# A hand-written planner for VectorE: exponential passes admitted by the next step's work, and side work held until the evacuation in front of it is due to end

## The chip, the core and the metric

The kernel runs on one core of a Trainium2 chip, as one launch. Its time is the device time of that launch in microseconds (us); for a kernel the median over its runs is given. The core's engines are TensorE (PE in the profile, its weight loads PEld), VectorE (DVE), ScalarE (ACT), GpSimd (POOL) and SyncE (SP); SP and POOL issue the DMAs.

## What is computed

Two rounds of an attention block and a token-mixing MLP, with residuals, on x of 2048 tokens by 640 features in bf16:

```python
def _A_ref(x, wqkv, wo):                 # H = 32 heads of 20
    qkv = transpose(reshape(x @ wqkv, (B, S, 3, H, Dh)), (2, 0, 3, 1, 4))
    q, k, v = qkv[0], qkv[1], qkv[2]
    scores = einsum("bhqd,bhkd->bhqk", q, k) * (Dh ** -0.5)
    o = einsum("bhqk,bhkd->bhqd", softmax(scores), v)
    return reshape(transpose(o, (0, 2, 1, 3)), (B, S, D)) @ wo

def _B_ref(x, w1, b1, w2, b2):           # mixes tokens: S = 2048, F = 1536
    u = gelu(einsum("bsd,sf->bdf", layernorm(x), w1) + b1)
    return transpose(einsum("bdf,fs->bds", u, w2) + b2, (0, 2, 1))

x = x + _A_ref(layernorm(x), wqkv, wo)
x = x + _B_ref(layernorm(x), w1, b1, w2, b2)
...                                      # both once more, same weights
```

The exponentials of the softmax are the bulk: 32 heads x 2048 x 2048 of them in each of the two attention blocks.

## The kernel before

**Score blocks and steps.** In `attention` (L257) a unit is a query block of 512 (qb, four of them), a group of four heads (g, eight) and a key block of 128 (kt, sixteen). A unit has four score blocks of 128 x 512, one for each head. Most of them get their exponential on ScalarE. Some get it on VectorE (`on_ve`, L290): all four of each group's last key block, and in some groups two of the one before, 166 blocks in each layer. A step is one tile of three score blocks in PSUM, in a pool with two buffers. It is either three blocks for ScalarE (a full step) or two for ScalarE and one for VectorE in the third place (a short step). There are 683 steps in each layer.

**The loop** (L751) is written out by hand and runs over the steps. In step t it emits the score matmuls of step t + 1 (`emit_S`, L441) and, if that step is short, VectorE's first read of the third block (`ve_first`, L351, tile ew). It then emits ScalarE's exponential of step t (`emit_exp`, L474, tile P), the multiplications with V of the units that are ready (`emit_PV`, L683, accumulator acc), the side work, and VectorE's passes. The order of TensorE's instructions is fixed to the order of emission. That of the other engines is not: the framework's scheduler puts together each engine's queue from what it reckons to be ready, with the emission order as priority.

**VectorE's exponential.** Two ew reads make a pair of 128 x 1024. `ve_enqueue` (L358) adds four passes for it to the list `ve_chain`: ey (L368, planned at 0.69 us), et (L374), Pd in its cubic form (L381) and Pd with the exponent added (L386), the last three planned at 1.22 us each. `ve_step` (L398), at the end of each step, advances a planned clock by the step's length (0.92 us for a short one, 1.344 for a full one) and emits passes from the list. The planner keeps `free`, the time until which VectorE is planned to be busy; every VectorE piece that the loop emits adds its cost to it (`dve_cost`, L345). A unit with blocks of VectorE has its multiplication with V deferred until its passes are planned to be done or nothing else is left; `ve_flush` (L411) then emits any pass still missing.

**Normalisation.** After the last unit of a group, `normalize` (L481) emits four VectorE instructions: a transpose out of the accumulator (T, L486), a reciprocal (rden), a product (T again) and a transpose into attnT (L493); it is planned at 2.4 us. The accumulator has one buffer, so the next group's first multiplication with V waits for the first transpose.

**Side work** is a queue of groups of matmuls that use one PSUM bank (tile misc, one buffer), each ended by a VectorE evacuation planned at 0.28 to 0.7 us: projections of keys and queries for later groups (L240, evacuated at L642 into KT and QTq), the output projection (L579, L614; evacuated at L589, L622 and L627 with the residual, into xin, x1s or x1last), and the part of the MLP's first product that belongs to the rows already finished (key "M", L551; evacuated at L557 into ustg and added to uacc in DRAM by a DMA that POOL issues, L560 and L562; its weights w1st are loaded by SP). `emit_fills` (L700) emits matmuls of it up to a budget a step; after each group it pauses for one step (`cooldown`). `planned_fill` (L730) tells at the start of a step whether there will be side work; if not, `keep_busy` (L460) emits matmuls with zero weights into the accumulator (L464). Side work that a group of heads needs at once is forced by `ensure_ready` (L663).

**After the loop** what is left of the side work is emitted with the score tile's pool as its bank (`tail_alloc`, L773). Then comes the layer norm of the last four row blocks (`emit_ln2_staged`, L520: statistics and nmr on VectorE, rstd on POOL at L182, hh on ScalarE and VectorE). `mixer_mm1` (L785) multiplies these rows (L826, tile big), adds uacc, which SP loads into ua (L809, four buffers), and `mixer_mm2` (L851) makes the second product from weights w2s (SP, L848), with x1in (SP, L886) as the residual.

Of the kernel before, what the change touches and what calls it, by code (L numbers as in the profile page):

```python
# [29 lines left out]
CFG = dict(  # L30
    SLOTS=4,
    FILL_NOPV=3.0,
    FILL_PV=1.5,
    PV_LAGT=1,
    PT_BUFS=4,
    FILL_GAP=1,
    KQ_AHEAD=1,
    A0_LAG=2,
    VE_SPACING=(2, 3),
    VE_LEAD=8,  # L40
    VE_SLACK=0.3,
)

LOG2E = 1.4426950408889634
# [8 lines left out]
def kernel(  # L53
# [203 lines left out]
    def attention(st, x_in_ap, x_mid, uacc_l):  # L257
        layer = st.layer
        KT, hT = st.KT, st.hT
        with ExitStack() as p1:  # L260
# [22 lines left out]
            fill_state = dict(cur=None, idx=0, tile=None, cooldown=0, unit=0)  # L283
# [11 lines left out]
            tiles, loc, last_tile = [], {}, {}  # L295
# [8 lines left out]
            while act_chunks or ve_left:  # L304
                t = len(tiles)
# [26 lines left out]
            NTILES = len(tiles)  # L332
            tile_left = {t: len(acts) for t, (acts, _) in enumerate(tiles)}
            pv_count = {}
            pv_plain = [deque() for _ in range(NU // NKT)]
            pv_mixed = [deque() for _ in range(NU // NKT)]
# [5 lines left out]
            ve_chain = deque()  # L342
            ve_clock = dict(now=0.0, free=0.0)

            def dve_cost(us):  # L345
                ve_clock["free"] = max(ve_clock["free"], ve_clock["now"]) + us
# [45 lines left out]
            def ve_next():  # L392
                p, cost, fn = ve_chain.popleft()
                fn()
                dve_cost(cost)
                ve_ready[p] = ve_clock["free"]

            def ve_step(us):  # L398
                ve_clock["now"] += us
                while ve_chain and ve_clock["free"] <= ve_clock["now"] + CFG["VE_SLACK"]:  # L400
                    ve_next()

            def ve_need(n):
# [41 lines left out]
            def emit_S(t):  # L445
                acts, ve = tiles[t]
                for (n, j) in acts:
                    if j == HORDER[0]:
                        on_unit_start(n)
                St = sps.tile([128, 3, 512], F32, name="S")  # L450
                S_tiles[t] = St
                for i, (n, j) in enumerate(acts):
                    s_matmul(St, i, n, j)
                if ve is not None:
                    if units[ve[0]][0:2] != units[acts[0][0] if acts else ve[0]][0:2]:
                        ensure_ready(*units[ve[0]][0:2])
                    s_matmul(St, 2, ve[0], ve[1])
                    ve_first(*loc[ve], St)

            def keep_busy(count):  # L460
                for acc in acc_tiles.values():
                    for _ in range(count):
                        for j in range(4):
                            pe(nc.tensor.matmul(acc[32 * j:32 * j + 32, :], lhsT=zw[:], rhs=zr[:].to_broadcast([128, 4, 128]), start=False,  # L464
                                                stop=False, skip_group_check=True, tile_position=(0, 32 * j)))

            def emit_exp(t):
                St = S_tiles.pop(t)
                ncs = len(tiles[t][0])
                if ncs == 0:  # L470
                    return
                P = ptp.tile([128, 3, 512], BF16, name="P")
                P_tiles[t] = P
                ex = nc.scalar.activation(out=P[:, 0:ncs, :].rearrange("p a b -> p (a b)"),  # L474
                                     in_=St[:, 0:ncs, :].rearrange("p a b -> p (a b)"),
                                     func=ACT.Exp, scale=SCALE)
                other = ve_reader.pop(id(St), None)
                if other is not None:
                    tc.declare_no_dep(ex.ins, other.ins, reason="both only read the score tile, in different banks")
# [191 lines left out]
            def emit_PV(n):  # L671
                qb, g, kt = units[n]
                done = pv_count.get((qb, g), 0)
                pv_count[(qb, g)] = done + 1
                if done == 0:
                    acc_tiles[(qb, g)] = accp.tile([128, 512], F32, name="acc")
                acc = acc_tiles[(qb, g)]
                ve_flush(n)
                for j in range(4):
                    ti, slot = loc[(n, j)]  # L680
                    P = ve_P[ti] if on_ve(n, j) else P_tiles[ti]
                    hh = 4 * g + j
                    pe(nc.tensor.matmul(acc[32 * j:32 * j + 32, :],  # L683
                                        lhsT=Vaug[:, (kt * H + hh) * VW:(kt * H + hh) * VW + 32],
                                        rhs=P[:, slot, :], start=(done == 0), stop=(done == NKT - 1),
                                        tile_position=(0, 32 * j)))
                    if not on_ve(n, j):
                        tile_left[ti] -= 1
                        if tile_left[ti] == 0:
                            del P_tiles[ti]  # L690
                if done == NKT - 1:
                    normalize(qb, g, acc_tiles.pop((qb, g)))
                    dve_cost(2.4)
                    if qb == LASTQB and PARTIAL_LAST:
                        if g % 2 == 1:
                            enqueue_outproj_partial(qb, g)
                    elif g == NG - 1:
                        enqueue_outproj(qb)

            def emit_fills(budget, pool_alloc):  # L700
                fs = fill_state
                if fs["cooldown"] > 0:
                    fs["cooldown"] -= 1
                    return 0.0
                spent = 0.0
                while spent < budget:
                    if fs["cur"] is None:
                        if not fill_queue:
                            break
                        if fill_queue[0].get("not_before", 0) > fs["unit"] and budget < 100:  # L710
                            break
                        fs["cur"] = fill_queue.popleft()
                        fs["idx"] = 0
                        fs["tile"] = pool_alloc()
                    grp = fs["cur"]
                    grp["mms"][fs["idx"]](fs["tile"])
                    spent += grp["cost"][fs["idx"]]
                    fs["idx"] += 1
                    if fs["idx"] == len(grp["mms"]):
                        grp["evac"](fs["tile"])  # L720
                        dve_cost(grp.get("dve", 0.69))
                        fs["cur"] = None
                        fs["cooldown"] = CFG["FILL_GAP"]
                        break
                return spent
# [2 lines left out]
                return miscp.tile([128, 512], F32, name="misc")  # L728

            def planned_fill():  # L730
                if fill_state["cooldown"] != 0:
                    return False
                if fill_state["cur"] is not None:
                    return True
                return len(fill_queue) > 0 and fill_queue[0].get("not_before", 0) <= fill_state["unit"]

            LAGT = CFG["PV_LAGT"]
            pv_group = 0

            def pv_next(t, n_pv):  # L740
                if pv_group >= len(pv_plain):
                    return None
                plain, mixed = pv_plain[pv_group], pv_mixed[pv_group]
                if plain and last_tile[plain[0]] <= t - LAGT:
                    return plain.popleft()
                if mixed and last_tile[mixed[0]] <= t - LAGT and len(plain) < NKT - 3:
                    if not plain or (n_pv == 0 and ve_done(mixed[0])):
                        return mixed.popleft()
                return None
            emit_S(0)  # L750
            for t in range(NTILES):  # L751
                has_fill = planned_fill()
                if t + 1 < NTILES:
                    emit_S(t + 1)
                emit_exp(t)
                n_pv = 0
                while (n := pv_next(t, n_pv)) is not None:
                    emit_PV(n)
                    n_pv += 1
                    if not pv_plain[pv_group] and not pv_mixed[pv_group]:  # L760
                        pv_group += 1
                short = len(tiles[t][0]) < 3
                if not has_fill:
                    keep_busy(CFG["SLOTS"] - 1 - n_pv - short)
                emit_fills(CFG["FILL_PV"] if n_pv or short else CFG["FILL_NOPV"], misc_alloc)
                ve_step(0.92 if short else 1.344)
            in_attention[0] = False
            while (n := pv_next(NTILES + LAGT, 0)) is not None:
                emit_PV(n)
# [245 lines left out]
```

## Time and profile before

| what | value |
|---|---|
| median of 3 runs | 2021.24 us (2020.55 to 2022.6) |
| the profiled execution | 2025.45 us, span 2023.7 us |
| mean granted TensorE clock | 0.975 |
| first attention loop, first start to last end of L474 | 49.6 to 931.5 us |
| second attention loop | 1052.6 to 1937.3 us |
| VectorE's passes L368, L374, L381, L386 | 166 of each; 0.69, 1.22, 1.21 and 1.21 us mean |
| ew, L351 | 332, 0.68 us mean |
| T out of the accumulator, L486 | 64, 0.71 us mean |
| zero matmuls, L464 | 5232 |

In the profile a group reads "line engine operation out<-in", count, busy time and mean duration of one in ns, and behind a second bar the idle time of its engine just before it, with what ended most of that. A wait reads "who <- for whom: total us, times, longest". A row of a timeline has its start and its duration in us; what stands in square brackets is the engine's idle time before it and what ended it. Durations come from one execution; matmul durations overlap, as one starts before the last has ended.

### The profile page before, as it was taken

The page shows a single profiled execution, that of the slowest core. Times are in us where ns is not written, and L with a number is a line of the kernel's source. Part 1 is how long each engine was busy: PE and PEld are TensorE (multiplying, and loading weights), DVE is VectorE, ACT ScalarE, POOL GpSimd, SP SyncE. Part 2 cuts the span into 40 slices and gives each one's busy share as a digit, 9 for nine tenths or more (in the row PEclk, how much of TensorE's full clock was granted, in tenths as well). Part 3 has the DMA queues.
Part 4 walks back from the last instruction along what each step waited for, and adds up shares of the span by engine and source line. Part 5 has one row for each costly group of instructions (what it writes and reads, how often), then busy time and mean ns, then how long its engine had stood idle before and what let it go on. Part 6 is the DMA issues. An engine that isn't in the chain of part 4 may idle for free.

```text
span 2023.7 us, 39147 instructions
## 1 busy us (share of the span) xinstructions
PE 1723.9 (85%) x16395; PEld 615.5 (30%) x16592; DVE 1388.9 (69%) x2091; ACT 1801.0 (89%) x1504; POOL 155.1 (8%) x220
## 2 busy tenths in 40 slices
PE   7888888888888887887998888888888888878879
PEld 4222222232222222223542222222222222222235
DVE  6777787666766577773557787777657765767742
ACT  5999999999999999996349999999999999999952
POOL 2000000110012001110000000001000220011000
PEclk9999999999999999998999999999999999999989
DMA  6000000110134012214620000112101430233145
GB/s 135 1 1 1 1 19 26 67 49 8 34 67 68 1 40 45 42 21 136 207 83 1 1 1 1 34 33 69 38 14 40 79 56 2 59 51 43 15 149 185
DMA packets 90768, 97.34 MB, mean 48 GB/s; under 512 B 9696, under 2 KB 68192, under 8 KB 90592
## 3 DMA queue, kind: packets, MB, share of 16 engines
q1 hardware_dynamic: 70464, 71.22, 11.3%
q0 software_dynamic: 20128, 23.62, 7.8%
q8 instruction: 129, 2.11, 0.4%
q14 instruction: 47, 0.39, 0.1%
HBM read 55.48 MB, written 39.32 MB: 47 GB/s over the span
## 4 chain that ended last, share of the span: by engine, by line
ACT 34%; PE 23%; DVE 22%; issue 19%; DMA 1%; POOL 0%; SPq 0%; another core or an unknown queue 0%; ACTq 0%; DVEq 0%; POOLq 0%
ACT P L474 34%; PE S L441 6%; PE y L897 5%; DVE ew L351 4%; PE acc L683 3%; DVE et L374 3%; DVE Pd L381 3%; PE acc L464 2%; DVE ey L368 2%; DVE Pd L386 2%; PE pp L231 2%; DVE T L486 1%; PE misc L551 1%; PE misc L240 1%; DVE T L491 1%
## 5 line engine op out<-in xcount | busy, mean ns | idle before, releaser
L474 ACT ACTIVATE P<-S 128x1536 bf16<-128x1536 f32 (+1 forms) x1366 | 1709.1, 1447 | 58.5 <-PE S L441 43.9
L441 PE MATMUL S<-QTq,KT 32*128 32x512 bf16 x4096 | 574.6, 388 | 198.9 <-ACT P L474 137.9
L683 PE MATMUL acc<-P,Vaug 128*32 128x512 bf16 x3764 | 388.9, 396 | 27.3 <-DVE T L486 26.6
L351 DVE TENSOR_SCALAR ew<-S 128x512 int32<-128x512 f32 x332 | 226.1, 681 | 262.6 <-PE S L441 262.3
L441 PEld LDWEIGHTS <-KT 32*128 32x128 bf16 x4096 | 195.9, 91 | 689.0 <-issue 539.0
L464 PE MATMUL acc<-zr,zw 128*32 128x512 bf16 x5232 | 404.4, 388 | 0.0
L374 DVE SCALAR_TENSOR_TENSOR et<-ey 128x1024 f32<-128x1024 f32 x166 | 202.5, 1220 | 4.4
L386 DVE SCALAR_TENSOR_TENSOR Pd<-ew,Pd 128x1024 int16<-128x1024 int16 x166 | 201.3, 1213 | 2.4
L381 DVE SCALAR_TENSOR_TENSOR Pd<-et,ey 128x1024 bf16<-128x1024 f32 x166 | 200.6, 1208 | 1.6
L683 PEld LDWEIGHTS <-Vaug 128*32 128x32 bf16 x4096 | 108.1, 93 | 278.3 <-issue 278.1
L464 PEld LDWEIGHTS <-zw 128*32 128x32 bf16 x5232 | 128.8, 97 | 97.2 <-issue 41.0
L557 DVE COPY ustg<-misc 128x512 f32<-128x512 f32 (+1 forms) x144 | 69.4, 482 | 109.1 <-PE misc L551 89.6
L182 POOL TENSOR_TENSOR rstd<-veps,mhalf 128x1 f32<-128x1 f32 x64 | 38.9, 608 | 1168.9 <-DVE veps L177 1049.7
L562 POOL DMA_DIRECT2D uacc<-ustg x96 | 86.2, 899 | 435.0 <-DVE ustg L557 421.6
L368 DVE TENSOR_SCALAR ey<-ew 128x1024 f32<-128x1024 uint16 x166 | 114.8, 692 | 2.9
L551 PE MATMUL misc<-h2st,w1st 128*128 128x128 bf16 (+1 forms) x512 | 104.7, 300 | 6.6 <-DVE ustg L557 5.3
L897 PE MATMUL y<-uT,w2s 128*128 128x128 bf16 (+1 forms) x754 | 106.8, 298 | 3.8 <-ACT uT L840 3.1
L240 PE MATMUL misc<-hh,wq_pad 128*128 128x512 bf16 x268 | 84.9, 384 | 6.2 <-DVE KT L642 2.5
L240 PE MATMUL misc<-hh,wk_pad 128*128 128x512 bf16 x250 | 78.6, 388 | 6.9 <-DVE KT L642 5.0
L486 DVE STREAM_TRANSPOSE T<-acc 128x512 f32<-128x512 f32 x64 | 45.5, 711 | 55.5 <-PE acc L683 55.5
L579 PE MATMUL misc<-wo_pad,attnT 128*128 128x128 bf16 (+1 forms) x362 | 73.6, 303 | 2.0 <-issue 1.0
L897 PEld LDWEIGHTS <-w2s 128*128 128x128 bf16 x768 | 59.7, 98 | 49.4 <-issue 4.6
(86 smaller groups left out, 898.8 us busy)
## 6 DMA issues: line engine op xcount, KB each, us to landing
uacc<-ustg POOLq DMA_DIRECT2D x72, 256.0 KB, 4.0
w2s<-in_B_w_dram SPq DMA_DIRECT2D x16, 768.0 KB
w1st<-in_B_w_dram SPq DMA_DIRECT2D x36, 256.0 KB
x1in<-xd SPq DMA_DIRECT2D x24, 320.0 KB
ua<-uacc SPq DMA_DIRECT2D x24, 320.0 KB
xd<-x2s SPq DMA_DIRECT2D x16, 320.0 KB
xin<-xd SPq DMA_DIRECT2D x16, 320.0 KB
uacc<-ustg POOLq DMA_DIRECT2D x72, 64.0 KB, 2.8
```

The lines of the kernel that those rows point to most:

```text
L240: pe(nc.tensor.matmul(t[:, :], lhsT=wpad[:, dt_, g, :], rhs=st.hT[:, dt_, tb * 512:(tb + 1) * 512], start=(dt_ == 0), stop=(dt_ == NDT - 1)))
L351: first = nc.vector.tensor_scalar(out=ve_w[p][:, slot, :], in0=St[:, 2, :], scalar1=ve_scale * 65536.0, scalar2=-127.0 * 65536.0, op0=ALU. ...
L368: nc.vector.tensor_scalar(out=y[:, 0:512 * k], in0=frac, scalar1=EXP_K / 65536.0, scalar2=EXP_K * (1.0 - EXP_ROOT), op0=ALU.mult, op1=ALU.add)
L374: nc.vector.scalar_tensor_tensor(out=box["t"][:, 0:512 * k], in0=y, scalar=EXP_P, in1=y, op0=ALU.add, op1=ALU.mult)
L381: nc.vector.scalar_tensor_tensor(out=box["P"], in0=box["t"][:, 0:512 * k], scalar=EXP_Q, in1=box["y"][:, 0:512 * k], op0=ALU.add, op1=ALU. ...
L386: nc.vector.scalar_tensor_tensor(out=bits, in0=whole, scalar=128.0, in1=bits, op0=ALU.mult, op1=ALU.add)
L441: pe(nc.tensor.matmul(St[:, slot, :], lhsT=KT[32 * j:32 * j + 32, g, kt * 128:(kt + 1) * 128], rhs=get_QT(st, qb)[32 * j:32 * j + 32, g, : ...
L464: pe(nc.tensor.matmul(acc[32 * j:32 * j + 32, :], lhsT=zw[:], rhs=zr[:].to_broadcast([128, 4, 128]), start=False, stop=False, skip_group_c ...
L474: ex = nc.scalar.activation(out=P[:, 0:ncs, :].rearrange("p a b -> p (a b)"), in_=St[:, 0:ncs, :].rearrange("p a b -> p (a b)"), func=ACT. ...
L551: pe(nc.tensor.matmul(t[:, 0:w], lhsT=states[fp]["w"][:, sti, ftl * 128:(ftl + 1) * 128], rhs=tiles4[sti][:, c0:c1], start=(sti == 0), sto ...
L683: pe(nc.tensor.matmul(acc[32 * j:32 * j + 32, :], lhsT=Vaug[:, (kt * H + hh) * VW:(kt * H + hh) * VW + 32], rhs=P[:, slot, :], start=(done ...
L897: pe(nc.tensor.matmul(y[:, 0:w], lhsT=w2s[:, ft, sl * 128:(sl + 1) * 128], rhs=uT[:, ft, c0:c1], start=(ft == 0), stop=(ft == NF - 1)))
```

## The change

Two things change in the planner; no operation on a tile is added or taken out.

First, `ve_step`. Before, a pass was emitted as long as VectorE's planned `free` time was at most 0.3 us ahead of the planned clock. Now a pass is emitted if its planned end, plus a reserve, lies within the next step's length plus 0.6 us. The reserve (`reserved_next`) is 0.69 us if the tile emitted in the next step has a block for VectorE, the evacuation's cost if the side-work group under way can end in that step, and 2.4 us if the group's last multiplication with V is due in it.

Second, `evac_pending`. When no side-work group is under way, and the evacuation of the last one is planned to end more than 0.2 us after the present planned time, `emit_fills` emits nothing (it returns ahead of the cooldown count), and `planned_fill` reports no side work, so that `keep_busy` takes its place. Forced side work and that after the loop are exempt, by their budget of 1000.

```diff
-    VE_SLACK=0.3,
+    VE_SLACK=0.6,
+    EVAC_SLACK=0.2,
...
-            def ve_step(us):
+            def ve_step(us, next_us, reserved):
                 ve_clock["now"] += us
-                while ve_chain and ve_clock["free"] <= ve_clock["now"] + CFG["VE_SLACK"]:
+                while ve_chain:
+                    begin = max(ve_clock["free"], ve_clock["now"])
+                    if begin + ve_chain[0][1] + reserved > ve_clock["now"] + next_us + CFG["VE_SLACK"]:
+                        break
                     ve_next()
...
+            def evac_pending():
+                return fill_state["cur"] is None and fill_state.get("evac_end", 0.0) > ve_clock["now"] + CFG["EVAC_SLACK"]
+
+            def reserved_next(t):
+                r = 0.0
+                if t + 2 < NTILES and tiles[t + 2][1] is not None:
+                    r += 0.69
+                cur = fill_state["cur"]
+                if cur is not None and sum(cur["cost"][fill_state["idx"]:]) <= CFG["FILL_NOPV"]:
+                    r += cur.get("dve", 0.69)
+                if pv_group < len(pv_plain):
+                    left = list(pv_plain[pv_group]) + list(pv_mixed[pv_group])
+                    if len(left) <= 2 and all(last_tile[n] <= t + 1 - LAGT for n in left):
+                        r += 2.4
+                return r
+
             def emit_fills(budget, pool_alloc):
                 fs = fill_state
+                if budget < 100 and evac_pending():
+                    return 0.0
                 if fs["cooldown"] > 0:
...
                         dve_cost(grp.get("dve", 0.69))
+                        fs["evac_end"] = ve_clock["free"]
                         fs["cur"] = None
...
             def planned_fill():
-                if fill_state["cooldown"] != 0:
+                if fill_state["cooldown"] != 0 or evac_pending():
                     return False
...
-                ve_step(0.92 if short else 1.344)
+                nshort = t + 1 < NTILES and len(tiles[t + 1][0]) < 3
+                ve_step(0.92 if short else 1.344, 0.92 if nshort else 1.344, reserved_next(t))
```

## The prediction

> **What bounds the kernel now.** I read the busy table first, then the groups, then who TensorE waits for, then single steps in order of time.
>
> ```profile
> span 2023.7 us, 39147 instructions
> ...
> PE 1723.9 (85%) x16395; PEld 615.5 (30%) x16592; DVE 1388.9 (69%) x2091; ACT 1801.0 (89%) x1504; POOL 155.1 (8%) x220
> ...
> L474 ACT ACTIVATE P<-S 128x1536 bf16<-128x1536 f32 (+1 forms) x1366 | 1709.1, 1447 | 58.5 <-PE S L441 43.9
> ```
>
> ScalarE's exponentials (L474, 1366 of them) set the pace: 1709 of 2024 us. They run in two loops, 49.6 to 931.5 us and 1052.6 to 1937.3 us by the first start and the last end of L474, together 1766.6 us. Undisturbed, the starts of two neighbours stand 1.33 us apart for three score blocks and 0.90 for two (medians of start-to-start). The forms count 1032 and 334, so the loops would take 1032 x 1.33 + 334 x 0.90 = 1673 us. **About 93 us are lost in the loops**, and this alone the change can win.
>
> The table of TensorE's waits (total us, times, longest) tells where:
>
> ```profile
> PE S L441 <- DVE ew L351: 36.2, 52, 1.4
> PE acc L683 <- DVE T L486: 26.6, 34, 2.0
> ...
> PE misc L614 <- DVE attnT L493: 9.2, 6, 2.3
> ...
> PE misc L240 <- DVE KT L642: 7.5, 14, 0.9
> PE misc L551 <- DVE ustg L557: 5.3, 7, 1.0
> ```
>
> Each row is TensorE held by a VectorE instruction that came late: the first read of a score block (ew, which frees the score buffer), the transpose that frees the accumulator (T), the evacuations of the one side-work bank (KT, ustg, and QTq with 2.1). With attnT they make 87 us. What a wait costs ScalarE I bound from both sides: its own idle time is 58.5 us, or 0.66 per us of wait; the 93 us lost are 1.05 per us. I take 0.85. Why more than the plain idle time is lost shows in two neighbouring windows (columns: busy us of the engines, then granted clock):
>
> ```profile
> 489.80:493.20 3.40, 1.81 (x24) 0.72 (x22) 3.37 (x4) 3.13 (x3) 0.00 (x0) 1.00 0.00 0
> 493.20:496.60 3.40, 3.40 (x26) 0.54 (x23) 3.16 (x6) 1.76 (x2) 0.00 (x0) 0.51 0.00 0
> ```
>
> TensorE waits 1.5 us for T in the first; in the second its clock is half, it is busy throughout, and ScalarE falls to 1.76 of 3.40. [...]
>
> **VectorE's passes (ve_step).** No instruction is added or removed: 166 groups of four passes either way. The planner emits them at other places, but VectorE's built order is not the emission order: the framework's scheduler also hoists a pass over a later-ready instruction. So I compared the built orders.
>
> *ew.* For each two neighbouring ew I added up what VectorE has between them by the row durations (0.69 for ey and ew, 1.22 for et and both Pd, 0.69 or 0.28 for an evacuation, 0.71 + 0.23 + 0.68 + 0.71 for a normalisation) and took away the steps between them (1.344 or 0.92 each). Before, 54 of the 330 pairs have a surplus over 1.25 us; these hold 42 of the 52 waits and 31.7 of the 36.2 us, 0.59 a pair. After, 28 pairs do: 28 x 0.59 = 16.4, plus 4.9 for the 302 others at the 4.5 us per 276 of before, gives 21. **ew -15 us of wait.** Ends: +2 (28 pairs at the longest wait, 1.36), and -33 (only the waits whose last three predecessors stay the same survive, 3.6 us).
>
> *T.* The plan reserves 2.4 us for a normalisation, to keep passes from in front of it. The built order does not follow:
>
> ```profile
> 326.29 0.69 DVE L368 TENSOR_SCALAR ey<-ew 128x1024 f32<-128x1024 uint16 x1
> 327.02 1.22 DVE L374 SCALAR_TENSOR_TENSOR et<-ey 128x1024 f32<-128x1024 f32 x1
> 328.17 0.71 DVE L486 STREAM_TRANSPOSE T<-acc 128x512 f32<-128x512 f32 x1
> ```
>
> This is a costly one: the next L683 then waited 1.20 us for T. Of 64 normalisations 34 have et directly in front before, 38 after, at the same steps; 23.5 us of the 26.6 lie behind an et, 0.69 each. **T +2**; ends -13 (half, if VectorE arrives with less backlog) and +15 (the ten that newly get an et pay 1.5 each).
>
> *attnT.* Two passes stand between T and attnT in 36 cases before and 40 after: 0, ends -3 and +3.
>
> **Side work that waits for its evacuation (evac_pending).** In the plan of before, 84 of 358 groups begin while their planned evacuation is still due; after, none of 352. That aims at KT, ustg, QTq and the small xin and x1s rows, 16 us. **-12**; ends 0 and -16. The wait is one of the planner, not of the chip: nothing queues behind it on TensorE; a held step has zero matmuls (L464) in place of side work. It holds in 200 steps; 120 zero matmuls of 5232 go, worth nothing where ScalarE sets the pace. The largest side work of one step stays eight matmuls, and the projections are never forced early in either plan. POOL's accumulating DMAs and SP's weight loads (w1st) slide with the side work; the cover is the 36 us that uacc waits at most for a next ustg (L562).
>
> The price is at the loop's end: **three groups per layer (one wide, two narrow) now run behind it.** Before, that stretch is:
>
> ```profile
> 940.98 0.56 POOL L182 TENSOR_TENSOR rstd<-veps,mhalf 128x1 f32<-128x1 f32 x1 [36.06 <-DVE veps L177]
> 942.29 0.55 POOL L182 TENSOR_TENSOR rstd<-veps,mhalf 128x1 f32<-128x1 f32 x1 [0.75 <-DVE veps L177]
> ...
> 944.19 1.22 PE L826 MATMUL big<-hh 128*128 128x512 bf16 x4 [4.13 <-ACT hh L193]
> ```
>
> The 12 matmuls fit into TensorE's 4.13 us of idle time. Three copies, 0.68 + 2 x 0.29 = 1.26 us, stand among the statistics that hh waits for; if their cover goes it is 1.26. POOL issues three DMAs between the four rstd, 0.9 each: up to 2.7, of which the later rstd hide about half behind the first of L826's four row blocks. On SP the x1in loads (320 KB) of the first layer now wait for the last accumulation and stand in front of eight of the ua loads, where DMA is 0.83 busy at 244 GB/s: two are 2.7 us. In the second layer the first four ua loads move behind a third w2s load. I take 3 us a layer, **+6**; ends +2.5 (the copies alone) and +13 (all three in full, (1.26 + 2.7 + 2.7) x 2).
>
> **Sum.** (-15 + 2 - 12) x 0.85 = -21, and +6: **-15 us**. The profiled execution took 2025.45 us (span 2023.7, 1.75 around it), so 2010; the median of the runs, 2021.24, is 4.2 lower: **2006 us**. Its own range is 1992 to 2015.
>
> **Rivals.**
> - *The order carries the plan after all*: passes also leave T. T -20, ew -29, evacuations -16, times 0.85, +6: -49, **1972 us**. For it: the plan's reserve. Against it: et in front of T in the built order, 38 times.
> - *The scheduler undoes it*: the change hardly does what it says. ew -3, evacuations -8, T +2, times 0.85, +6: -2, **2019 us**. For it: the same patterns, cu and ex in front of ew, stay in many groups of the last three query blocks.
> - *T gets worse, and the kernel slower.* Place: normalisations 19 and 25 to 28 of each layer, counted from 0, where ey directly in front of T gives way to et. Price: 1.5 us of wait, and a half-clock stretch behind it that costs another 1.2 (ScalarE is busy 1.76 us in the window above and 3.02 in the one after it): 10 x 2.7 = +27. With ew -13, evacuations -10 and +6 that is +10, **2031 us**. It decides from the seventh of the ten on (19 against the net gain of 17 from the rest). Against it: 18 of the 34 with et in front wait less than 0.3 us or not at all now.
>
> **Chances.** Forecast 0.52, order carries the plan 0.08, undone 0.20, T worse 0.20. About 0.2%, or 4 us, is what a measurement of this kernel can tell from no change. Faster: 0.51 of the forecast, 0.08, and 0.06 of the undone case, 0.65. Same: 0.01 and 0.12, 0.13. Slower: 0.20 and 0.02, 0.22. The range reaches from the forecast's low end, stretched for ew's far bound, to the T case: 1988 to 2032.
>
> **What would show it.** In the waits of the changed kernel: S behind ew near 21 us in some 35 waits, KT, ustg and QTq together under 4, T near 28 and still behind et; the two loops shorter by some 10 us each; fewer half-clock windows in them; three ustg copies among the statistics after each loop and L826 starting 1 to 3 us later after the last L474. I am wrong if T falls below 15 or rises above 38, if ew stays above 30, or if the loops shorten and the stretches behind them take it back by more than 12.

## The result, and the profile after

The changed kernel takes 2047.4 us (median of four runs, 2042.4 to 2050.4), the kernel before, run beside it on the same chip, 2021.9 us. The ratio is **1.0118, interval 1.0091 to 1.0146: slower by 1.2%, or 25 us**, where the prediction said 2006. The profiled execution took 2042.4 us (span 2040.6), against 2025.5 (span 2023.7) before, so the two traces show 17 of the 25 us: the traced execution of the kernel before lies 4 us above its median, that of the changed kernel 5 us below.

The page of the changed kernel, its busy table and the group of the exponentials:

```profile
span 2040.6 us, 38886 instructions
...
PE 1733.8 (85%) x16251; PEld 617.1 (30%) x16472; DVE 1390.5 (68%) x2091; ACT 1801.8 (88%) x1504; POOL 159.1 (8%) x220
...
L478 ACT ACTIVATE P<-S 128x1536 bf16<-128x1536 f32 (+1 forms) x1366 | 1710.1, 1451 | 64.8 <-PE S L445 50.8
```

ScalarE does the same work (1710 us); its idle time grew from 58.5 to 64.8 us. By stages, cut at the first start and the last end of the exponentials of each loop and at the first start of the matmuls into big behind it:

| stage (us) | before | after |
|---|---|---|
| two loops | 881.9 + 884.7 | 884.3 + 889.5 |
| last exponential to first matmul into big | 12.7 + 13.2 | 19.1 + 15.6 |
| everything else | 231.2 | 232.2 |

So by these two traces 7.2 us were lost in the loops, which were to become 21 us shorter, and 8.8 behind them; by the medians the loops' part would be some 16. Who TensorE waited for in the changed kernel (total us, times, longest):

```profile
PE S L445 <- DVE ew L352: 31.1, 58, 2.1
PE acc L687 <- DVE T L490: 30.7, 32, 2.2
PE misc L618 <- DVE attnT L497: 11.5, 6, 2.3
PE big L850 <- ACT hh L194: 9.7, 2, 6.6
PE misc L241 <- issue: 7.5, 46, 0.3
PE S L618 <- DVE attnT L497: 4.5, 2, 2.3
PE misc L555 <- DVE ustg L561: 3.7, 7, 0.7
...
PE misc L555 <- issue: 3.2, 17, 0.3
PE misc L241 <- DVE KT L646: 3.1, 10, 0.5
...
PE misc L583 <- issue: 1.7, 11, 0.2
...
PE misc L241 <- DVE QTq L646: 0.9, 2, 0.5
```

The waits for ew fell by 5 us, those for the evacuations (KT, ustg, QTq) from 14.9 to 7.7. But T rose by 4 us in nearly as many waits, and attnT by 2. The three "issue" rows (the engine waited for nothing that the profile shows) add up to 12.4 us, 4.1 before, but they are most likely no waits: this trace has 16251 matmul records beside 16472 weight loads, so 221 are missing, 91 of them of L241; the same side work shows no such row in the trace with the edge on T further down, which has all 16472. All of TensorE's waits behind VectorE in the two loops fell from 88.6 to 81.4 us only. At the same time the stretches of the loops with TensorE's clock under 0.9 grew **from 72 to 99 us**.

The normalisation that the prediction showed at 328.17 us stands here half a microsecond earlier, and is dearer (time order, VectorE and the matmul that waits):

```profile
325.75 0.69 DVE L369 TENSOR_SCALAR ey<-ew 128x1024 f32<-128x1024 uint16 x1
...
326.47 1.23 DVE L375 SCALAR_TENSOR_TENSOR et<-ey 128x1024 f32<-128x1024 f32 x1
327.62 0.71 DVE L490 STREAM_TRANSPOSE T<-acc 128x512 f32<-128x512 f32 x1
328.25 1.18 DVE L382 SCALAR_TENSOR_TENSOR Pd<-et,ey 128x1024 bf16<-128x1024 f32 x1
328.38 0.40 PE L687 MATMUL acc<-P,Vaug 128*32 128x512 bf16 x4 [1.93 <-DVE T L490]
```

et is again directly in front of T, and L687 waits 1.93 us where L683 waited 1.20. The windows around it (busy us of PE, PEld, DVE, ACT, POOL, then granted clock):

```profile
326.90:330.30 3.40, 1.92 (x10) 0.42 (x9) 3.40 (x5) 2.08 (x3) 0.00 (x0) 0.91 0.00 0
330.30:333.70 3.40, 3.34 (x24) 0.99 (x23) 3.29 (x6) 2.94 (x3) 0.00 (x0) 0.50 0.00 0
333.70:337.10 3.40, 3.40 (x22) 0.71 (x20) 2.26 (x5) 2.66 (x3) 0.00 (x0) 0.50 0.15 58
```

The two windows behind the wait are at half clock, and TensorE is nearly or wholly busy in them; ScalarE idles 0.46 and 0.74 us there, beside 1.32 in the window of the wait. Over both loops, ScalarE's idle time inside half-clock stretches rose from 18.7 to 25.5 us; outside them it fell from 37.3 to 35.8.

Behind the first loop, VectorE's copies into ustg, POOL's transfers and the layer norm, in time order:

```profile
944.90 0.29 DVE L561 COPY ustg<-S 128x128 f32<-128x128 f32 x1
945.49 0.89 POOL L566 DMA_DIRECT2D uacc<-ustg  x1 [0.29 <-DVE mv L175]
946.61 0.69 DVE L561 COPY ustg<-S 128x512 f32<-128x512 f32 x1 [0.94 <-PE S L555]
...
952.11 0.29 DVE L561 COPY ustg<-S 128x128 f32<-128x128 f32 x1 [3.44 <-DMA uacc<-ustg]
952.43 0.16 DVE L192 TENSOR_SCALAR nmr<-mv,rstd 128x1 f32<-128x1 f32 x1
...
952.63 1.73 ACT L194 ACTIVATE hh<-x1last,nmr,rstd 128x640 bf16<-128x640 f32 x2 [18.13 <-DVE nmr L192]
...
953.60 1.22 PE L850 MATMUL big<-hh 128*128 128x512 bf16 x4 [6.60 <-ACT hh L194]
```

ustg has two buffers. The third copy needs the first one back, whose transfer into uacc has not landed, and it waits 3.44 us for it at the head of VectorE's queue. nmr, which hh needs, stands behind it. The prediction counted the copy (0.29 us) and not this wait.

### The profile page after: what moved, and what is told of

It is laid out like the page before. It is cut to its first block, busy times and chain, and to the rows that moved or that the text cites. A ratio compares the mean times of both kernels' runs of the same rounds, so it can differ in the third digit from the quotient of the medians.

```text
span 2040.6 us, 38886 instructions
## 1 busy us (share of the span) xinstructions
PE 1733.8 (85%) x16251; PEld 617.1 (30%) x16472; DVE 1390.5 (68%) x2091; ACT 1801.8 (88%) x1504; POOL 159.1 (8%) x220
## 4 chain that ended last, share of the span: by engine, by line
ACT 35%; PE 23%; DVE 20%; issue 20%; DMA 1%; POOL 1%; SPq 0%; ACTq 0%; DVEq 0%; POOLq 0%
ACT P L478 35%; PE S L445 6%; PE y L921 5%; DVE ew L352 4%; PE acc L687 3%; DVE et L375 3%; DVE Pd L382 2%; PE acc L468 2%; DVE ey L369 2%; PE misc L241 2%; DVE Pd L387 2%; PE pp L232 2%; DVE T L490 1%; PE misc L555 1%; PE big L850 1%
## 5 line engine op out<-in xcount | busy, mean ns | idle before, releaser
L478 ACT ACTIVATE P<-S 128x1536 bf16<-128x1536 f32 (+1 forms) x1366 | 1710.1, 1451 | 64.8 <-PE S L445 50.8
L687 PE MATMUL acc<-P,Vaug 128*32 128x512 bf16 x3764 | 390.2, 397 | 31.5 <-DVE T L490 30.7
L468 PE MATMUL acc<-zr,zw 128*32 128x512 bf16 x5112 | 399.5, 390 | 0.0
L687 PEld LDWEIGHTS <-Vaug 128*32 128x32 bf16 x4096 | 107.7, 93 | 285.6 <-issue 285.6
L183 POOL TENSOR_TENSOR rstd<-veps,mhalf 128x1 f32<-128x1 f32 x64 | 44.2, 699 | 1037.4 <-DVE veps L178 918.2
L241 PE MATMUL misc<-hh,wq_pad 128*128 128x512 bf16 x264 | 87.7, 398 | 6.5 <-issue 3.4
L241 PE MATMUL misc<-hh,wk_pad 128*128 128x512 bf16 x242 | 75.7, 383 | 5.7 <-issue 4.1
L646 DVE CAST QTq<-misc 128x512 bf16<-128x512 f32 x62 | 42.4, 685 | 54.9 <-PE misc L241 54.5
```

The source lines that it names most:

```text
L241: pe(nc.tensor.matmul(t[:, :], lhsT=wpad[:, dt_, g, :], rhs=st.hT[:, dt_, tb * 512:(tb + 1) * 512], start=(dt_ == 0), stop=(dt_ == NDT - 1)))
L687: pe(nc.tensor.matmul(acc[32 * j:32 * j + 32, :], lhsT=Vaug[:, (kt * H + hh) * VW:(kt * H + hh) * VW + 32], rhs=P[:, slot, :], start=(done ...
```

## The experiments

**Theory**: both parts cost. The hold leaves groups for behind the loop, and VectorE's built order puts passes in front of T whatever the planner emits. What made me look there: in the order in which the changed planner emits VectorE's work, 58 of 64 normalisations come straight behind an ew and only two behind a pass; in the built order 38 come behind et. **Rivals**: the hold makes all of it; the pass rule makes all of it; waits only move from one instruction to another.

### Either part alone, and the loop's end without the hold

The pass rule alone:

```diff
-    EVAC_SLACK=0.2,
+    EVAC_SLACK=100.0,
```

> The new rule for VectorE's passes alone; side work never waits for an evacuation (its slack is set so high that it never holds), so no group of side work runs behind the loops. Theory 1 (the loss is made by both parts: about 9 us behind the loops by the three held-back groups a layer, the rest in the loops by passes that get in front of T): the 9 us go and the loops keep T at 30 us of wait or more, 2028 to 2036 us. Theory 2 (the hold makes all of it, the pass rule is neutral): 2018 to 2024 us. Theory 3 (the pass rule makes all of it): 2042 us or more.

Measured: 2018.8 us, ratio 0.9991 (0.9977 to 1.0006). No difference from before that shows: **theory 2 of that expectation** (the hold makes it). T even fell:

```profile
PE S L445 <- DVE ew L352: 36.7, 57, 1.4
PE acc L687 <- DVE T L490: 21.6, 28, 2.0
```

but ew stands at 36.7, where it was before (36.2), with the same 10 waits over 1 us, 12.4 us in all. The rule that was to bring ew down does not by itself.

The hold alone (old `ve_step`, `VE_SLACK` 0.3, `evac_pending` kept):

```diff
-                while ve_chain:
-                    begin = max(ve_clock["free"], ve_clock["now"])
-                    if begin + ve_chain[0][1] + reserved > ve_clock["now"] + next_us + CFG["VE_SLACK"]:
-                        break
+                while ve_chain and ve_clock["free"] <= ve_clock["now"] + CFG["VE_SLACK"]:
                     ve_next()
```

> The hold of side work alone, with the old rule and the old slack for the passes. Three groups a layer are again left for the stretch behind the loop. Theory 1 (both parts): +9 behind the loops, -5 in them from earlier evacuations, 2024 to 2032 us. Theory 2 (the hold makes all of it): 2042 us or more. Theory 3 (the pass rule makes all of it): 2018 to 2024 us.

Measured: 2053.3 us, ratio 1.0155 (1.0129 to 1.0181). Again theory 2, and mine fell: with the old rule the hold costs 32 us, more than both parts together. 8.8 of them are the stretches behind the loops (19.3 + 15.5 us); the loops are 21 us longer (1787.6). Part of that is a thing which neither of the two full kernels has. This is the hold alone, about 247 us into the trace:

```profile
247.69 1.24 PE L241 MATMUL misc<-hh,wq_pad 128*128 128x512 bf16 x5 [0.78 <-DVE KT L643]
248.86 0.39 PE L442 MATMUL S<-QTq,KT 32*128 32x512 bf16 x1
248.96 0.69 DVE L643 CAST QTq<-misc 128x512 bf16<-128x512 f32 x1 [1.33 <-PE misc L241]
249.71 0.39 PE L442 MATMUL S<-QTq,KT 32*128 32x512 bf16 x2 [0.46 <-DVE QTq L643]
...
250.19 3.71 ACT L475 ACTIVATE P<-S 128x1536 bf16<-128x1536 f32 x3 [2.13 <-PE S L442]
```

The projections have slid so far that five of their matmuls are issued at once, the score matmuls wait for QTq, and ScalarE idles 2.13 us. The planner forces 56 matmuls in this way, both layers together, at six steps of each layer's first query block.

The changed kernel, with no hold in the last 60 of the 683 steps:

```diff
             def evac_pending():
-                return fill_state["cur"] is None and ...
+                return step_now[0] < NTILES - 60 and fill_state["cur"] is None and ...
```

> The changed kernel, but in the last 60 of the 683 steps of a layer side work is not held back: 8 fewer held steps a layer, and no group of the feed-forward part is left behind the loop. Theory 1: the stretches between the last exponential and the first matmul into big go back from 19.1 and 15.6 us to about 12.7 and 13.2, everything else stays: 2047 - 9 = 2038 us. Rival (the loops make the loss and the stretches give what they took to the stage behind them): 2044 us or more.

Measured: 2031.9 us, ratio 1.0052 (1.0030 to 1.0074). Both stretches are back (13.1 and 13.0 us) and the loops stay (1774.2 against 1773.8). The three groups were worth 15 us by the medians, more than the 9 expected and than the 8.6 that the stretches of the two traces show. Most of the difference is which execution was traced: the traced ones are 10.9 us apart (2042.4 and 2031.5), 8.6 of them in the stretches. The other 10 us or so to the kernel before are in the loops.

### T ahead of the passes that are emitted behind it

An ordering edge on VectorE's queue, without a semaphore, from every pass to the last T emitted before it:

```diff
+            def after_T(inst):
+                if last_T[0] is not None:
+                    tc.add_manual_dep(inst.ins, last_T[0].ins.name, mybir.DependencyInfo(
+                        mybir.DependencyClass.NoSync, mybir.DependencyReason.DATA), reason="behind the transpose")
+                return inst
...
-                nc.vector.transpose(out=T1[:], in_=acc[:])
+                last_T[0] = nc.vector.transpose(out=T1[:], in_=acc[:])
```

and each of the four passes is wrapped in `after_T(...)`. On the changed kernel:

> The changed kernel, with one constraint on VectorE's order: a pass that the planner emits behind the transpose T of a normalisation is not built in front of it. No instruction is added. In the planner's own order no normalisation but two comes straight behind a pass; in the built order of the changed kernel 38 of 64 had et directly in front of T, with this constraint none. Theory 1 (the built order undoes the plan, and waits for T are what the loops lose): the wait of TensorE for T falls from 30.7 to under 12 us, half-clock time in the loops from 99 to under 75 us, and the time to 2020 to 2033 us. Rival (the passes then stand in front of something else, ew or attnT or the evacuations, and the sum of waits stays): waits for T fall as well, but the time stays over 2040 us. Third possibility (T is reached late for another cause, the ew or the evacuation ahead of it): T stays over 20 us.

Measured: **1994.0 us, ratio 0.9866 (0.9845 to 0.9888)**: 53 us off the changed kernel, and faster than the kernel before, by no new instruction (the page counts 221 more than that of the changed kernel, the matmul records that are missing there).

```profile
span 1991.7 us, 39107 instructions
...
PE 1744.9 (88%) x16472; PEld 616.3 (31%) x16472; DVE 1382.6 (69%) x2091; ACT 1795.8 (90%) x1504; POOL 153.7 (8%) x220
...
L486 ACT ACTIVATE P<-S 128x1536 bf16<-128x1536 f32 (+1 forms) x1366 | 1704.2, 1485 | 24.4 <-PE S L453 14.5
```

Its waits:

```profile
PE S L453 <- DVE ew L360: 29.4, 54, 1.8
...
PE acc L695 <- DVE T L498: 4.3, 18, 0.4
...
PE misc L626 <- DVE attnT L505: 1.7, 5, 0.3
```

T fell from 30.7 to 4.3 us, attnT from 11.5 to 1.7, and of the rest only the waits for xin and x1s rose, to 3.4 together; half-clock time in the loops is 41 us, the loops 1727.5. 36 us of waits went and the loops became 46 us shorter. Theory 1 holds and was too careful (2020 to 2033). The normalisation from above now waits for its matmuls, not for a pass:

```profile
324.21 0.69 DVE L360 TENSOR_SCALAR ew<-S 128x512 int32<-128x512 f32 x1
...
325.23 0.40 PE L695 MATMUL acc<-P,Vaug 128*32 128x512 bf16 x4
325.69 0.72 DVE L498 STREAM_TRANSPOSE T<-acc 128x512 f32<-128x512 f32 x1 [0.78 <-PE acc L695]
...
326.46 0.40 PE L695 MATMUL acc<-P,Vaug 128*32 128x512 bf16 x4
```

VectorE idles 0.78 us for the accumulator, and the next accumulation waits for nothing.

### The same edge in the other three versions, and both repairs together

> The kernel before, old pass rule, no hold, with the one constraint that a pass emitted behind the transpose T of a normalisation is not built in front of it. Theory 1 (what VectorE's built order puts in front of T is the dear thing, whatever the plan): TensorE's wait for T falls from 26.6 to under 8 us, the time to 1992 to 2004 us. Theory 2 (the constraint pays because the new pass rule has planned room for T; the old rule itself emits a pass straight in front of 30 of 64 normalisations, which the constraint leaves there): T stays over 13 us, 2007 to 2018 us.

> The new pass rule and the constraint on T, without the hold. Without the constraint this was 2018.8 us, and the constraint took 53 us from the changed kernel. Theory A (with T in its place the hold is worth nothing in the loops and only costs behind them): 1975 to 1988 us, KT, QTq and ustg waits of 13 to 16 us. Theory B (the hold does shorten the loops once T is in its place): over 1990 us.

> The hold and the constraint on T, with the old pass rule. Without the constraint 2053.3 us. If T's place is what matters in every variant, it falls by 25 us or more, to under 2028 us. If the constraint needs the new rule's plan, it stays over 2040 us.

> The changed kernel with the constraint on T and without the hold in the last 60 steps of a layer: both repairs. If they add up (-53 and -15): 1979 us. If the stretch behind the loop pays less now: 1985 to 1992 us. A version that beats the kernel before by 1.5% or more in either case.

Measured, with the versions without the edge beside them (loops, T and half-clock in the loops from the profiled executions, us). Each ratio is to the kernel before on the same chip, from all runs and not from the two medians; the median of before was 2021.9 for the change, 2021.1 for the other rows without the edge and for "both + edge", and 2019.2 for the other rows with it:

| version | median | ratio, interval | loops | T | half clock |
|---|---|---|---|---|---|
| before | 2021 | 1 | 1766.5 | 26.6 | 72 |
| pass rule alone | 2018.8 | 0.9991 (0.9977 to 1.0006) | 1757.6 | 21.6 | 48 |
| hold alone | 2053.3 | 1.0155 (1.0129 to 1.0181) | 1787.6 | 27.1 | 102 |
| both (the change) | 2047.4 | 1.0118 (1.0091 to 1.0146) | 1773.8 | 30.7 | 99 |
| both, no hold at the end | 2031.9 | 1.0052 (1.0030 to 1.0074) | 1774.2 | 30.1 | 106 |
| before + edge | 1987.4 | 0.9832 (0.9808 to 0.9857) | 1729.8 | 4.3 | 27 |
| pass rule + edge | 1986.8 | 0.9832 (0.9807 to 0.9857) | 1729.0 | 5.3 | 21 |
| hold + edge | 2017.0 | 0.9986 (0.9972 to 0.9999) | 1753.2 | 6.3 | 55 |
| both + edge | 1994.0 | 0.9866 (0.9845 to 0.9888) | 1727.5 | 4.3 | 41 |
| both, no hold at the end, + edge | **1981.1** | **0.9812 (0.9787 to 0.9836)** | 1722.9 | 3.9 | 31 |

Three things follow.
- The edge takes 32 to 53 us in every version (36 from the hold alone, where 25 or more were expected), and both repairs together come within 2 us of their sum (1979). On the kernel before it does so too: T falls as theory 1 said, and the time lies below its range (1992 to 2004). The old rule emits a pass in front of 30 of the 64 T by itself, and these cost little (T 4.3). The dear ones were those that the scheduler had hoisted. So the new pass rule, with the room that it plans for a normalisation, is worth nothing that shows: 0.6 us with the edge, 2.3 without.
- The hold's 16 us in the loops (1757.6 to 1773.8, pass rule in both) are gone with the edge (1729.0 to 1727.5). They came by way of T: 21.6 to 30.7 us without the edge, 5.3 to 4.3 with it. With the edge, and off at the end of the loop, the hold is worth 6 us (1986.8 to 1981.1, four and five runs), all of it in the loops (1729.0 to 1722.9). So the run without the hold came out in theory A's range (1986.8), but that the hold is worth nothing in the loops did not hold; KT, QTq and ustg were 17.9 us there, more than the 13 to 16 expected.
- Under the old rule the hold costs 30 us with the edge and 32 without, 23 and 21 of them in the loops. Here T is not the cause.

### The forced projections, and the third copy

The hold with the old rule and the edge, but not in the first 171 steps of a layer:

```diff
             def evac_pending():
-                return fill_state["cur"] is None and ...
+                return step_now[0] >= 171 and fill_state["cur"] is None and ...
```

> The constraint on T and the hold with the old pass rule, as in the run at 2017.0 us, but no hold in the first 171 of 683 steps of a layer (the first query block). There the hold with the old rule lets the projections slide until 56 of their matmuls have to be issued at six steps a layer, ahead of the score matmuls that need them; now none is. Theory 1 (these forced projections are what the hold costs in the loops under the old rule): the loops come back from 1753 us to the 1730 of the same kernel without any hold, and what is left is the stretch behind the loop, 8 to 15 us: 1995 to 2003 us. Rival (the held steps themselves cost it): over 2010 us.

Measured: 1997.7 us, ratio 0.9884 (0.9858 to 0.9909), loops 1731.1 us. Theory 1: the 22 us between 1753 and 1731 are the first query block's, where the projections were forced. That it was the forcing and not the held steps of that block was not tried apart; what speaks for it is the version with both parts and the edge, which holds side work there too, forces nothing, and has loops of 1727.5 us. So the one use of the new pass rule that shows is that with it the hold doesn't push the projections over their last moment.

The three copies behind each loop into tiles of the exponentials' pool, so that the third waits for no transfer:

```diff
-                                stg = ustg.tile([128, 512], F32, name="ustg")
+                                if in_attention[0]:
+                                    stg = ustg.tile([128, 512], F32, name="ustg")[:]
+                                else:
+                                    stg = ptp.tile([128, 3, 512], BF16, name="P")[:, 0:2, :].rearrange(
+                                        "p a b -> p (a b)").bitcast(F32)
```

> The changed kernel, but the three copies into ustg behind each loop go to tiles of the exponentials' pool, which is free by then, so none waits for an earlier accumulating transfer out of the two ustg buffers. The three groups, their matmuls, copies and transfers stay behind the loop. Theory 1 (the third copy's 3.44 us of wait for the transfer, ahead of the layer norm on VectorE, is the larger part of the stretch's growth in the first layer): that stretch falls from 19.1 to 15.0 to 16.0 us, the second layer's stays at 15.6 (its third copy waited for no transfer), 2041 to 2045 us. Rival (the transfers issued from POOL between the rstd make it, 0.9 each): both stretches stay within 0.7 us of 19.1 and 15.6.

Measured: 2042.9 us, ratio 1.0098 (1.0065 to 1.0132). The stretch of the first layer fell from 19.1 to 15.5 us, that of the second stayed (15.4): theory 1.

```profile
951.95 0.29 DVE L565 COPY P<-S 128x128 f32<-128x128 f32 x1
952.54 0.89 POOL L570 DMA_DIRECT2D uacc<-P  x1 [0.36 <-DVE mv L175]
953.65 0.89 DVE L565 COPY P<-S 128x512 f32<-128x512 f32 x2 [0.94 <-PE S L555]
954.65 1.75 POOL L570 DMA_DIRECT2D uacc<-P  x2 [1.22 <-DVE veps L178]
955.83 0.20 DVE L192 TENSOR_SCALAR nmr<-mv,rstd 128x1 f32<-128x1 f32 x1
...
957.04 0.59 PE L854 MATMUL big<-hh 128*128 128x512 bf16 x1 [3.06 <-ACT hh L194]
```

The second and third copy now follow each other without a wait for a transfer, and nmr comes 14.3 us behind the loop (955.83, the loop ending at 941.55) in place of 17.9. What is left of the growth is 2.8 us in this layer and 2.2 in the second, with the groups' own work and POOL's three transfers in it; how it divides was not tried.

### Two more constraints on the order, on the fastest version

A second edge of the same kind keeps passes behind each ew. For both of the following kernels the passes of the pair that still holds ew's buffer are emitted ahead of the ew that needs it, so each changes two things:

```diff
                 if slot == 0:
+                    while ve_chain and ve_chain[0][0] <= p - 2:
+                        ve_next()
                     ve_w[p] = vew.tile([128, 2, 512], I32, name="ew")
...
+                last_T.append(first)
...
-                if last_T[0] is not None:
+                for before_ in (last_T[0], last_T[-1]):
```

> The fastest version so far (1981.1 us: changed kernel, T constraint, no hold in the last 60 steps) with a second constraint of the same kind: a pass emitted behind an ew is not built in front of it. For this the passes of the pair that still fills ew's buffer are emitted ahead of the ew. If passes hoisted over ew make its waits (31.8 us in 60 waits, two of them over 2 us and followed by half-clock windows): ew under 22 us, 1962 to 1974 us. If ew's waits come from the passes emitted ahead of it, or are hidden behind ScalarE: 1976 to 1986 us. If passes now reach the PV matmuls late: over 1990 us.

Measured: 1987.3 us, ratio 0.9826 (0.9800 to 0.9852), against 0.9812 without it. ew falls from 31.8 us in 60 waits to

```profile
PE S L457 <- DVE ew L363: 17.3, 16, 1.6
```

but not the time: the loops are 7 us longer, and the score matmuls wait 5.9 us for QTq, which they did not before. The wait is as the first possibility said; the time lies 1.3 us above the range of the second and fits none.

The whole order of VectorE in the loops chained to the order of emission, in place of the edge on T:

```diff
+            def dv(inst):
+                tc.chain_iter_dep("dve_order", inst.ins)
+                return inst
...
-                first = nc.vector.tensor_scalar(
+                first = dv(nc.vector.tensor_scalar(
```

and so for the passes, the normalisations and the evacuations.

> The same version, with VectorE's whole order in the loops (ew, passes, normalisations, evacuations; not the layer norm's) chained to the order of emission, in place of the constraint on T. The passes of the pair that still fills ew's buffer are emitted ahead of the ew here too. If the plan is good as it stands and the built order alone spoils it: 1965 to 1980 us, ew under 25 us. If the scheduler's other moves do good (an instruction that is ready in place of one that is not), it stands at 1985 to 2010 us with more waits for evacuations and attnT, still faster than the changed kernel, since T is in its place.

Measured: 2019.4 us, ratio 0.9985 (0.9969 to 1.0002), beyond both expectations. T is low, but other waits took its place:

```profile
PE S L451 <- DVE ew L358: 46.1, 62, 2.0
...
PE S L451 <- DVE QTq L652: 8.5, 12, 1.5
PE acc L693 <- DVE T L496: 6.6, 18, 0.7
...
PE misc L561 <- DVE ustg L567: 6.0, 6, 1.5
```

So the plan is not good as it stands: with all of the scheduler's moves undone the kernel is 38 us slower than with only the one over T undone (1981.1). Some 6 us of that may come from the passes emitted ahead of ew, as in the run before. The scheduler's other moves help, taken together, and the one over T hurts.

## Why the prediction was wrong

- **What bounds the kernel** was right: in all fourteen traces the two loops less ScalarE's idle time come to 1700 to 1715 us, and the versions differ in how long ScalarE idles in them (56.0 us before, 61.3 in the change, 22.0 with the edge on T). The 93 us lost there were not all to be had by the change, but 44 of them are gone in the fastest version (1766.5 to 1722.9).
- **0.85 us per us of wait: failed, and with it the sum of -21. This step decided the sign in the loops.** Waits behind VectorE fell by 7 us in place of 25; at 0.85 these 7 would still have won 6, and the loops became 7 longer. (Over the 87 us that the prediction names, its two bounds are 0.67 and 1.07.) The price took all waits as alike; those that went were short, those that came long: waits over 1.5 us went from 8 to 14, and 27 us more of half-clock time came with them. ScalarE's idle time fell by 1.5 us outside the half-clock stretches and rose by 6.8 inside.
- **ew -15: failed**, measured -5; 31.1 us is above the 30 that the prediction named as a sign of being wrong. I counted pairs of neighbouring ew with a surplus over 1.25 us in the built order, and priced them at 0.59. The long waits went (over 1 us: 10 waits with 12.4 us before, 2 with 4.2 after); the short ones grew. The count held for the long waits alone, and for both parts together only.
- **T +2**: measured +4. The 38 et in front of T cost 25.5 us, 0.67 each, where 34 cost 23.5: this part was right, in number and in price. What it left out is the 17th normalisation (from 0) of each layer, where h2st, the layer norm's piece for a finished row block, now stands in front of T in place of et, and the wait went from 0.00 to 1.06 us. Nor were the et "at the same steps": three a layer lost theirs (the 8th, 16th and 17th), and five got one. The even mean also hid that the waits became longer: the 9th went from 1.20 to 1.93 us, the 12th from 0.91 to 1.17, the 24th from 1.95 to 2.22, the 27th from 0.58 to 1.58, and waits over 1 us from 14 (19.9 us) to 20 (28.5). It is the hold that did this: with the pass rule alone the 9th, 12th, 17th and 27th stand at 0.84, 0.40, 0.00 and 0.58.
- **attnT 0**: measured +2, within its end of +3.
- **Evacuations -12**: measured -8 with the small rows; KT, ustg and QTq stand at 7.7 us, not under 4. That no projection is forced was right for the change, and only thanks to the new pass rule.
- **Tail +6**: 8.8 in the traces. The named parts were there (copies, POOL's transfers). The largest, 3.44 us for the third copy's buffer, was not priced, though the waits of the kernel before have VectorE's ustg copies held by such a transfer three times, 10.6 us.
- **Rivals.** "T gets worse, and the kernel slower" (2031) came nearest in kind and sign, but not in place: of its five normalisations only the 27th paid, others that I had not named did. That its sign came out is in part luck. Its sum also takes the gains of the rest at their full wait; at 0.85 it is 2035. What speaks for it is that T in its place takes the loss in the loops away. It was weighed against a net gain of 17 us from the rest, and that gain was too high: ew gave 5 of 13, the evacuations 8 of 10. "The order carries the plan" (1972) is refuted in both ways: the order didn't carry it, and when it was made to, the time was 2019.4.
- **The clock.** The waits that half clock followed were short in the changed kernel too: the first window shown above has 1.48 us idle of 3.40 (1.93 in the clock's own step, see the last section), the row that the prediction shows 1.59, and none of TensorE's waits behind VectorE in the loops is longer than 2.3 us.

Still open: how the loss in the loops by the medians (some 16 us) divides, as the traces hold only 7 of it.

## What to carry to other kernels

A plan that places instructions on an engine is worth what the built order keeps of it: compare the order of emission with the built one around the instruction that frees the next resource (here T, which frees the only accumulator), and pin that one instruction rather than all. Test the parts of a change apart before refining either: here one part did nothing, the other cost time, and an edge that adds no instruction was worth more than both were meant to bring. Work that is postponed must still be paid for where the plan ends, there with whatever ring of buffers it brings along. And a price per us of wait holds only while the waits keep their length.

## What the runs showed of the hardware that was not expected

The kernel whose copies behind the loop have their own buffers has the same instructions in the same order on TensorE, VectorE and ScalarE as the changed kernel up to the end of each loop, and the same waits there (T 30.6 and 30.7, ew 30.8 and 31.1). Yet in its profiled execution the loops took 1783.5 us against 1773.8, with 130 us at half clock against 99. So a like wait does not always bring a half-clock window, and in this pair each microsecond at half clock went with about 0.3 us of time (9.7 of 30.7). The mean granted clocks of the two executions are 0.960 and 0.966.

In the traces of the kernel before and of the changed kernel, the 17 and 23 half-clock stretches of the loops begin on one grid of 3.41 us and, like the one of three such steps from 329.70 to 339.94 us in the changed kernel, last whole steps of it. In the step ahead of that one, from 326.29 to 329.70, no matmul runs for 1.93 us. Ahead of all 40 stretches, that time is 1.16 to 2.29 us in the step; but steps with up to 1.62 us (before) and 1.79 us (changed) were followed by full clock, and as both traces lack matmul records, these times can be too long. A wait that crosses a grid line is split between two steps. The wait of the 15th normalisation (from 0) of 1.55 us lies inside one step in the changed kernel, and half clock followed; in the kernel whose copies have their own buffers it is 1.54 us long with a grid line in it, and none followed.
